# A fixed order list for every engine in place of a ranked greedy scheduler, with larger first loads, moved buffers, and sums and copies made by DMA

## The chip, the core and the metric

The kernel runs on one core of a Trainium2 chip. The metric is the device time of one execution in microseconds (us). Of the core's engines, TensorE (PE) does matrix products, VectorE (DVE) element-wise work, ScalarE (ACT) functions of one operand and copies out of PSUM, and GpSimd (POOL) and SyncE (SP) mostly issue DMAs. Each engine executes its instructions strictly in the order in which they were written; it waits on semaphores for the work of the others.

## What is computed

Two independent layers share one kernel, and their outputs are joined along the last axis. All inputs are bfloat16; S = L = 2048, D = 448, 16 heads of 28, 256 states.

```python
# A: linear attention with a softmax feature map
q, k, v = split_heads(x @ wqkv)
pq, pk = q @ w_phi, k @ w_phi                     # per head, 28 x 28
phi = lambda p: concat(softmax(p), softmax(-p))
kv, z = einsum(phi(pk), v), sum(phi(pk))
a = (phi(pq) @ kv / (phi(pq) @ z + 1e-6)) @ wo

# B: state-space convolution over the sequence
dt = exp(log_dt)
P = exp(dt * (A_re + 1j * A_im) * l)              # l = 0..2047, as bfloat16
K = einsum(C, P, dt * B).real                     # (448, 2048)
y = irfft(rfft(pad(u)) * rfft(pad(K)))[:2048] + u * Dskip
out = concat(a, y)
```

## The kernel before

**The work.** Layer B sets most of it. The raw state parameters (six tensors of 448 x 256) are turned to states on partitions (`to_states`: PE transposes, ACT copies to `st`). From them come the powers `PW[k]` for steps of 32, 64, 128, 256, 512 and the table `H` of start values. The positions l are split into 50 low and 32 high parts. Eight chunks of 56 channels each go through `chunk(k)` and `table(k)`: ACT computes exponentials (`exps`, into `E`) and sines (`rot`, into `W`) for the low parts; DVE multiplies them (`damp`), negates (`neg`), and builds the high parts in `U` from `H` by repeated complex products (`hi_tables`, levels hi.1 to hi.5); PE contracts the two (`build`), and a copy out of PSUM writes the table `Ts`. `E`, `W` and `U` have two halves, one for even and one for odd chunks. `scatter_k` moves a finished group of tables (chunks 0-3, 4-5, 6-7) into `Kt` with 48 small DMAs. `kernel_spectrum` (ks) transforms `Kt` with matrices `F` that stream from memory through a ring of buffers. `signal_spectrum(b)` (us) loads sequence half b of u twice, once by `rep_rows` and once, with rows in reverse, by `pair_rows`, forms sums and differences on DVE (`ab`), transforms them with `G1` on PE, and stores the spectrum to `SUd` in device memory, from where `load_su` fetches it. `conv_group` multiplies the two spectra on DVE (prod, comb, half) and `inverse` transforms back on PE with the constants `GI`, adding `UD`, the input scaled by Dskip. Layer A (`xT`, `fold`, `key_pair`, `key_end`, `query`) fills the gaps: its key pass runs beside chunks 0 to 4, its query pass beside the later ones.

**The order.** Every operation is a unit of a `Plan`: the engines that may run it, its estimated cost, what it reads and writes. `Plan.run` then plays the whole program with these costs. At each step it takes the engine that can start soonest and, of the units that could start there within 0.02 us, the one with the lowest number in `RANKS`, a table by label. `PHASES` keeps ACT's exponentials and sines apart, since a change of function loads a table. Copies out of PSUM may go to ACT or DVE, some DMAs to SP or POOL or ACT, PSUM tiles to one of two rings: the simulated race decides. What comes out is one list of instructions per engine.

**Lines and names used below.** All DVE two-operand instructions are issued in one helper (L429), activations in another (L442), copies in L446 (ACT only) and L452 (either engine), matrix products in L462, DMAs in L477; so the profile's groups are told apart by shape. `ua` and `ab` hold the loaded and the summed signal; `SUs`, `SKs`, `GI`, `UD`, `RING` are the late buffers and share bytes with earlier ones (`oU`, `oE`, `oPID`, `oF`, `oW` are the offsets).

Of the kernel before, what the change touches and what calls it, by code (L numbers as in the profile page):

```python
# [94 lines left out]
def rep_rows(x2, row, a, t):  # L95
    rs = x2.ap[0][0]
    return bass.AP(tensor=x2.tensor, offset=x2[row + 256 * t + 128 * (1 - a), 0].offset,
                   ap=[[2 * rs, 64], [1, D_MODEL]])

def pair_rows(x2, row, t, col):  # L100
    rs = x2.ap[0][0]
    return bass.AP(tensor=x2.tensor, offset=x2[row + 1023 - 128 - 256 * t, col].offset,
                   ap=[[128 * rs, 2], [-2 * rs, 64], [1, D_MODEL]])

RANKS = {"in": 5, "inAre": 52, "inAim": 281, "inCre": 30, "inBre": 135, "inCim": 122, "inBim": 213, "inx0": 266,
         "inx1": 145, "inx2": 100, "inx3": 168, "inqk": 114, "inG": 265, "inv_": 282, "one": 93, "pid": 190, "bd":
# [42 lines left out]
class Plan:  # L149


    LAT = {"PE": 0.28, "DVE": 0.15, "ACT": 0.16, "POOL": 0.2, "SP": 0.0}
    SLACK = 0.02
    WINDOW, COLUMNS = 3.4133, 3030

# [4 lines left out]
    def step(self, label, base, phase=None):  # L160

        self.now, self.base = label, self.ranks.get(label, base)
        return self.phases.get(label, phase)
# [68 lines left out]
    def run(self):  # L232
# [24 lines left out]
        def ring(x):  # L257

            best = None
            if x.need:  # L260
                return None
# [902 lines left out]
```

## Time and profile before

| | us |
|---|---|
| three runs | 336.96, 340.40, 339.19 |
| median | 339.19 |
| the profiled execution | 341.56 |
| its span, first to last instruction | 339.8 |
| mean granted TensorE clock in it (share of full) | 0.947 |
| DMA traffic in the span | 32.87 MB |

An execution of the profile is read in three ways here: by stages (busy time of each engine in a stretch of the span), by groups (all instructions of one line and shape: count, busy time in sum, mean in ns, idle time of the engine just before them), and in order of time (start, length, engine, line, what it writes and reads, and in brackets the idle time before it and who ended it). The mean of a group can be longer than busy time over count, since instructions of one engine overlap at their ends. For DMAs the queues' names are SPq, ACTq and POOL. Instructions that only issue DMAs are not counted as busy time on SP and ACT.

The page's row of DMA activity, in 40 equal slices (tenths of the 16 DMA engines' time):

```profile
DMA  8993001121020011200203031225369766589014
```

The first four slices (to 34 us) carry the first loads, the right third the `F` stream, the scatters and the stores.

### The profile page before, as it was taken

Reading aid. Unit: us, or ns where it says so; the run is one execution under the profiler, and the core shown is the slowest. Engines: PE = TensorE matmul, PEld = TensorE weight load, DVE = VectorE, ACT = ScalarE, POOL = GpSimd, SP = SyncE. Lnnn points to the kernel's source line nnn. Section 1 sums busy time; section 2 is a strip of 40 time slices with the busy share of each in tenths; the row PEclk is TensorE's granted clock in tenths of the full one; section 3 lists DMA queues with packets and bytes.
Section 4 is the critical chain, followed back from the end, with each engine's and each line's share of the span. In section 5 each row is a group of like instructions: output and inputs, shape, how many; then the busy total and the mean of one; then the engine's idle time right before and its main releaser. Section 6 shows DMA issues by size and latency. Waiting matters only on the chain. (4 is left out here: it accounts for less than half of the span.)

```text
span 339.8 us, 9802 instructions
## 1 busy us (share of the span) xinstructions
PE 266.4 (78%) x4193; PEld 211.0 (62%) x4193; DVE 295.0 (87%) x337; ACT 256.0 (75%) x486; POOL 48.5 (14%) x95
## 2 busy tenths in 40 slices
PE   1465766889877978989989989998679970699993
PEld 1355444546754745657777766796557960599983
DVE  0369999999999995999999999999999649959991
ACT  2789999999997978999999998999973200152420
POOL 3000000100010000000019400006900027500000
PEclk9999995999999997999999999999979976599998
DMA  8993001121020011200203031225369766589014
GB/s 164 281 303 85 0 2 50 48 84 64 31 88 23 4 56 54 109 3 3 77 12 28 10 95 43 71 70 139 54 168 245 204 194 139 132 265 246 6 56 164
DMA packets 42540, 32.87 MB, mean 97 GB/s; under 512 B 20993, under 2 KB 41890, under 8 KB 42112
## 3 DMA queue, kind: packets, MB, share of 16 engines
q1 hardware_dynamic: 36643, 30.41, 30.7%
q0 software_dynamic: 2624, 0.64, 2.0%
q10 hardware_dynamic: 3229, 1.19, 1.9%
q8 instruction: 33, 0.54, 0.7%
q14 instruction: 11, 0.09, 0.1%
HBM read 24.28 MB, written 7.34 MB: 93 GB/s over the span
## 5 line engine op out<-in xcount | busy, mean ns | idle before, releaser
L462 PEld LDWEIGHTS <-sbuf 128*32 128x32 bf16 (+5 forms) x4049 | 196.6, 122 | 99.7 <-issue 47.4
L429 DVE TENSOR_TENSOR sbuf<-sbuf 128x448 bf16<-128x448 bf16 (+9 forms) x225 | 234.4, 1085 | 24.6 <-ACT sbuf L446 13.9
L462 PE MATMUL mm<-sbuf 128*32 128x50 bf16 (+9 forms) x1923 | 146.0, 285 | 24.2 <-ACT sbuf L452 12.5
L442 ACT ACTIVATE sbuf<-arg 128x448 bf16<-128x448 f32 (+3 forms) x216 | 114.6, 709 | 0.7 <-PE arg L462 0.5
L462 PE MATMUL kb<-sbuf 128*32 128x50 bf16 (+7 forms) x1416 | 78.4, 255 | 23.7 <-DMA sbuf<-const 13.2
L452 ACT CAST sbuf<-mm 128x448 bf16<-128x448 f32 (+3 forms) x81 | 48.0, 611 | 30.3 <-PE mm L462 21.2
L477 POOL DMA_DIRECT2D sbuf<-sbuf x73 | 41.1, 590 | 108.5 <-ACT sbuf L452 41.9
L462 PE MATMUL arg<-sbuf 128*128 128x112 bf16 (+1 forms) x710 | 45.6, 220 | 0.8 <-DVE sbuf L429 0.5
L452 ACT CAST sbuf<-kb 128x448 bf16<-128x448 f32 (+4 forms) x42 | 23.4, 579 | 22.2 <-PE kb L462 20.6
L442 ACT ACTIVATE sbuf<-mm 128x448 bf16<-128x448 f32 (+1 forms) x60 | 31.0, 598 | 3.1 <-PE mm L462 2.8
L442 ACT ACT_TABLE_LOAD x14 | 18.0, 1283 | 6.3 <-DMA sbuf<-in_B_A_re_dram 6.0
L641 PE MATMUL kb<-sbuf 128*112 128x128 bf16 x64 | 8.2, 286 | 11.5 <-ACT sbuf L452 6.2
L822 DVE TENSOR_REDUCE sbuf<-sbuf 128x64 f32<-128x1792 bf16 x8 | 16.1, 2012 | 0.0
L641 PEld LDWEIGHTS <-sbuf 128*112 128x112 bf16 x64 | 7.6, 191 | 13.4 <-issue 8.6
L442 ACT ACTIVATE sbuf<-sbuf 128x896 f32<-128x896 f32 (+1 forms) x11 | 12.3, 1127 | 0.3 <-DVE sbuf L429 0.3
L429 DVE TENSOR_TENSOR sbuf<-kb,sbuf 128x448 bf16<-128x448 f32 (+3 forms) x23 | 11.8, 531 | 0.7 <-PE kb L462 0.7
L452 DVE CAST sbuf<-kb 128x448 bf16<-128x448 f32 (+2 forms) x6 | 3.6, 605 | 9.5 <-PE kb L462 9.4
L452 DVE CAST sbuf<-mm 128x448 bf16<-128x448 f32 (+4 forms) x18 | 10.5, 594 | 1.5 <-PE mm L462 1.2
L452 ACT COPY sbuf<-kb 112x512 bf16<-112x512 bf16 (+1 forms) x16 | 9.0, 602 | 3.4 <-PE kb L641 3.2
L452 ACT CAST sbuf<-arg 128x224 bf16<-128x224 f32 (+1 forms) x12 | 4.3, 396 | 9.0 <-PE arg L462 9.0
L569 PE MATMUL mm<-sbuf 112*128 112x112 bf16 x48 | 5.5, 295 | 5.9 <-ACT sbuf L442 2.6
L766 ACT ACTIVATE sbuf<-sbuf 128x1680 bf16<-128x1680 bf16 x6 | 9.8, 1641 | 0.0
(33 smaller groups left out, 70.5 us busy)
## 6 DMA issues: line engine op xcount, KB each, us to landing
sbuf<-const SPq DMA_DIRECT2D x36, 224.0 KB
SUd<-sbuf SPq DMA_DIRECT2D x16, 224.0 KB
sbuf<-const SPq DMA_DIRECT2D x3, 1024.0 KB
sbuf<-in_A_x_dram SPq DMA_DIRECT2D x4, 448.0 KB
out_dram<-sbuf SPq DMA_DIRECT2D x16, 112.0 KB
sbuf<-in_B_u_dram SPq DMA_DIRECT2D x4, 448.0 KB
sbuf<-SUd SPq DMA_DIRECT2D x2, 896.0 KB
sbuf<-SUd SPq DMA_DIRECT2D x1, 1792.0 KB
```

The costliest lines, as they stand in the source:

```text
L429: lambda: nc.vector.tensor_tensor(out=at(out_), in0=at(a), in1=at(b), op=op), [whose(a), whose(b)], [out_])
L442: lambda: nc.scalar.activation(at(out_), at(a), func, scale=scale, bias=bias),
L452: lambda e: (nc.scalar.copy if e == "ACT" else nc.vector.tensor_copy)(at(out_), at(a)), [whose(a)], [out_])
L462: nc.tensor.matmul(out_, lhsT=lhsT, rhs=rhs, start=start, stop=stop, **kw)
L477: plan.add({e: own[e] for e in engs}, lambda e=engs[0]: QUEUES[e].dma_start(out=out_, in_=in_), r, w, lat=lat, load=pieces / 16000 * max(2 ...
L569: mms(p, [lambda t, nch=nch, j=j: nc.tensor.transpose(t[:, nch, 112 * j:112 * j + 112], raw[nm][:, j, 128 * nch:128 * nch + 128], id112) f ...
L641: mms(p, [lambda t, j=j, x=x: nc.tensor.transpose(t[:, j, :], x[:, 112 * j:112 * j + 112], ident[:, :]) for j in range(4)], 0.4, [x, ident ...
L766: lambda en: nc.scalar.mul(m, m, -1.0) if en == "ACT" else nc.vector.tensor_scalar_mul(m, m, -1.0), [m], [m])
L822: plan.add({"DVE": 1.93}, lambda: nc.vector.tensor_reduce(zk, EK.rearrange("p i s (h f) -> p (i s h) f", f=D_HEAD), axis=AX.X, op=ALU.add) ...
```

## The change

- `Plan.run` no longer simulates. `ORDER` lists all 1389 units by number with one letter for the engine (P, V, A, G for POOL, S), in the order in which they are written; `PLACES` names the PSUM ring of each of 291 tiles. Ranks, phases and costs no longer choose anything. In the new list ACT makes nearly all copies out of PSUM (24 casts on DVE become 8), POOL issues 92 of the 144 scatter pieces (73 before), and six DMAs that ACT issued at the start become one.
- First loads: the raw state tensors are loaded with four neighbouring rows per partition (2048 contiguous bytes instead of 512), x likewise (3584 instead of 896). Rows then sit at other places, so `to_states` picks every fourth column, and the store of layer A's output takes every fourth row.
- `to_states` uses plain matrix products with the identity into float32 PSUM; for the two A tensors DVE multiplies straight out of PSUM by dt, with no copy between.
- `signal_spectrum`: per half two row loads go straight into `ab[:, 0]` and four pair loads into `ua`; one DVE instruction of 1792 columns forms the difference, and a DMA of POOL adds `ua` onto `ab[:, 0]` in place (`accum_op`). Before, four steps of three loads and two DVE instructions of 448 columns each.
- `hi_tables`: the copy of `H` into the first rows of `U` is a DMA; the first product reads `H` itself.
- Homes: `SU0` moves from `U` to `H`; `SU2`, `SK0`, the products `Y`, the sums `S` and a temporary `s2` move; the `F` ring has seven slots of 1792 bytes per partition (six before), of which two lie in a buffer of the key pass.

```diff
-def rep_rows(x2, row, a, t):
+def rep_rows(x2, row, a):
     rs = x2.ap[0][0]
+    return bass.AP(tensor=x2.tensor, offset=x2[row + 128 * (1 - a), 0].offset, ap=[[2 * rs, 64], [256 * rs, 4], [1, D_MODEL]])
...
-def pair_rows(x2, row, t, col):
+def pair_rows(x2, row, t):
     rs = x2.ap[0][0]
+    return bass.AP(tensor=x2.tensor, offset=x2[row + 1023 - 128 - 256 * t, 0].offset,
                    ap=[[128 * rs, 2], [-2 * rs, 64], [1, D_MODEL]])
...
+ORDER = ("0A 15G 22P 23A 24A 1S 2S 27P 28V 25P 26V 36A 16G 6S 3S 4S 29P 30V 31P 32V 37V 33A 35A 38A 34A 165S 59P 60V 12S "
+         "139P 140V 39V 166S 164S 167S 44A 43A 40A 41A 51P 57P 58V 123P 18G 143P 5S 163S 162S 124V 52V 144V 168V 45V 9S "
...
     def run(self):
+        places, done = iter(PLACES), set()
+        for word in ORDER.split():
+            u, e = self.units[int(word[:-1])], ENGINES[word[-1]]
+            assert e in u["costs"] and u["deps"] <= done
             for x in u["ps"]:
                 if x.t is None:
+                    x.make(TAGS[next(places)])
             if len(u["costs"]) > 1:
                 u["fn"](e)
             else:
                 u["fn"]()
+            done.add(u["n"])
...
-        dma(["SP", "ACT"], raw[nm][:, :, :], srcs[nm].rearrange("(j p) n -> p j n", p=112), w=[raw[nm][:, :, :]])
+        dma(["SP"], raw[nm][:, :, :], srcs[nm].rearrange("(p j) n -> p j n", j=4), w=[raw[nm][:, :, :]])
...
-            acopy(states(st[nm])[:, nch], (p, lambda t, nch=nch: channels(t[:, nch, 0:D_MODEL])))
+            p = ps("mm", [128, 512])
+            mms(p, [lambda t, j=j: mm(t[:, j:D_MODEL:4], raw[nm][:, j, 128 * nch:128 * nch + 128], id112, True, True)
+                    for j in range(4)], 0.375, [raw[nm][:, :, :], ident[:, :]], act=392)
+            use(nch, (p, lambda t: channels(t[:, 0:D_MODEL])))
...
-        tt(f[:, :], st[nm][:, :], dtx[:, :], ALU.mult)
+        to_states(nm, 10 + i, lambda nch, a: tt(states(f)[:, nch], a, states(dtx)[:, nch], ALU.mult))
...
-            tt(ab[:, 0, t, :], ua[:, 0, :], ua[:, 1, :], ALU.add)
-            tt(ab[:, 1, t, :], ua[:, 0, :], ua[:, 1, :], ALU.subtract)
+            dma(["SP"], ua[:, t, :], pair_rows(u2, 1024 * b, t), w=[ua[:, t, :]], lat=5, cost=0.85)
+        step(f"ab{b}.0", rank)
+        tt(ab[:, 1], ab[:, 0], ua[:, :, :], ALU.subtract)
+        step(f"ab{b}.1", rank)
+        dma(["POOL"], ab[:, 0], ua[:, :, :], r=[ab[:, 0], ua[:, :, :]], w=[ab[:, 0]], lat=5, cost=0.85, accum_op=ALU.add)
...
-        copy(u[:, 0:4], H[:, :, :, cols], 0.41e-3)
+        dma(["SP", "POOL"], u[:, 0:4], H[:, :, :, cols], r=[H[:, :, :, cols]], w=[u[:, 0:4]])
...
-    SUs = [group_tile("SU", i, o) for i, o in enumerate((oU, oE + 14336, oPID + 29184))]
-    SKs = [group_tile("SK", i, o) for i, o in enumerate((oF + 7168, oU + 14336, oU + 21504))]
+    SUs = [group_tile("SU", i, o) for i, o in enumerate((oH, oE + 14336, oW + 36288))]
+    SKs = [group_tile("SK", i, o) for i, o in enumerate((oF + 5376, oU + 14336, oU + 21504))]
...
-    oY, oS, oTT = oPID, oPID + 14336, (oE, oW + 21952)
-    RING = [oF + 1792 * i for i in range(4)] + [oEND, oEND + 1792]
+    oY, oS, oTT = oU, (oPID, oPW), (oE, oW + 21952)
+    RING = [oF + 1792 * i for i in range(3)] + [oEND, oEND + 1792, oEK, oEK + 1792]
```

The list's order at the places that the prediction speaks of, by counting the units in the order of the code: SP starts with the identity, the raw states Are, Cim, Aim, Cre, a pair load, Wqk, three pair loads, Bre, two row loads of u, a quarter of x, Bim. DVE's thirteenth unit is the difference of u's first half, followed by the products cs32 and cs128. ACT's copy of the power 128 (pw128) follows the copies of Bre, two of x and Bim. DVE has hi.5's two sums between the two products of damp7, then skip0 and the first product of conv0. PE runs the two builds of table 7, then the rest of the queries, mixed with the spectra of groups 0 and 1 and the first inverse; then group 2's spectra, and the inverses of the three groups.

More of the change, by code (lines that the diff above doesn't have):

```diff
@@ L182, in add @@
     def add(self, costs, fn, r=(), w=(), phase=None, lat=None, gate=None, mode=0, load=0, act=None):
[L184 to L185 removed]
+        u = dict(costs=costs, fn=fn, n=len(self.units), deps=set(), ps=[])
         self.units.append(u)
@@ L190, in add @@
                     if x not in u["ps"]:
-                        if not x.users and x.order is not None:
-                            self.orders.setdefault(x.tags[0], []).append((x.order, len(self.units), x))
                         u["ps"].append(x)
@@ L232, in run @@
-    def run(self):
-        units = self.units
-        left, table, wire, lanes = {}, None, 0.0, {True: [0.0] * 8, False: [0.0] * 8}
-        free = {e: 0.0 for e in self.LAT}
-        ready = {e: [] for e in self.LAT}
-        pe = {"warm": False, "win": -self.WINDOW, "act": 0.0, "mode": 0}
-        for u in units:
-            u["wait"], u["at"] = len(u["deps"]), 0.0
-            for m in u["deps"]:
-                units[m]["kids"].append(u)
-            if u["phase"] is not None:
-                left[u["phase"]] = left.get(u["phase"], 0) + 1
-        for u in units:
-            if not u["wait"]:
-                for e in u["costs"]:
-                    ready[e].append(u)
-        turn = {tag: [x for _, _, x in sorted(o, key=lambda z: z[:2])] for tag, o in self.orders.items()}
-        for u in units:
-            for x in u["ps"]:
-                if not x.long:
-                    for m in u["deps"] - x.users - x.need:
-                        x.need.add(m)
-                        units[m].setdefault("opens", []).append(x)
[L257 to L261, printed above, removed]
-            if x.order is None or turn[x.tags[0]][0] is x:
-                for tag in x.tags:
-                    r = self.rings.setdefault(tag, [])
-                    if len(r) < x.bufs or not r[-x.bufs].users:
-                        t = r[-x.bufs].end if len(r) >= x.bufs else 0.0
-                        if best is None or t < best[0]:
-                            best = (t, tag)
-            return best
-        def start(u, e, first):
-            t = max(u["at"], free[e])
-            for p in (u["gate"], u["phase"]):
-                if p is not None and p > first:
-                    return None
@@ L276, in start @@
+    def run(self):
+        places, done = iter(PLACES), set()
+        for word in ORDER.split():
+            u, e = self.units[int(word[:-1])], ENGINES[word[-1]]
+            assert e in u["costs"] and u["deps"] <= done
             for x in u["ps"]:
                 if x.t is None:
-                    place = ring(x)
-                    if place is None:
-                        return None
-                    t = max(t, place[0])
-            return max(t, lanes[e == "POOL"][-8]) if u["load"] else t
@@ L317, in run @@
                 u["fn"]()
-            free[e] = t + cost
-            end = t + cost + (u["lat"] or self.LAT[e])
-            if u["load"]:
-                wire = max(wire, t + 0.5 * cost + 0.25) + u["load"]
-                end = max(wire + 1.1, t + cost + (u["lat"] or 0.0))
-                lanes[e == "POOL"].append(end)
-            for x in u["ps"]:
-                x.users.discard(u["n"])
-                x.end = max(x.end, end)
-            for x in u.get("opens", ()):
-                x.need.discard(u["n"])
-            for v in u["kids"]:
-                v["wait"] -= 1
-                v["at"] = max(v["at"], t + cost if e == "PE" and e in v["costs"] else end)
-                if not v["wait"]:
-                    for k in v["costs"]:
-                        ready[k].append(v)
+            done.add(u["n"])
+        assert len(done) == len(self.units)
 class Ps:
@@ L603 @@
     for i, nm in enumerate(RAW[2:]):
-        to_states(nm, 20 + i)
+        to_states(nm, 20 + i, lambda nch, a: copy(states(st[nm])[:, nch], a))
     step("cb", 24)
```

117 lines of the change are left out of this document (33 added, 84 removed), and 103 rows, old and new, of tables (ORDER, PHASES, RANKS).

## The prediction

> **What bounds the kernel now.** I read the page first, then the stretches of the span, then the head and the tail in order of time.
>
> ```profile
> span 339.8 us, 9802 instructions
> PE 266.4 (78%) x4193; PEld 211.0 (62%) x4193; DVE 295.0 (87%) x337; ACT 256.0 (75%) x486; POOL 48.5 (14%) x95
> ```
>
> ```profile
> 0.00:27.00 27.00, 11.31 (x97) 9.51 (x98) 10.35 (x13) 17.15 (x29) 3.55 (x11) 1.00 0.95 253
> 27.00:247.00 220.00, 184.78 (x2862) 136.57 (x2862) 212.18 (x260) 211.66 (x405) 31.84 (x61) 0.97 0.18 49
> 247.00:252.10 5.10, 3.62 (x26) 2.61 (x23) 5.10 (x4) 5.10 (x8) 0.05 (x1) 0.78 0.43 105
> 252.10:331.00 78.90, 63.37 (x1147) 59.18 (x1148) 66.14 (x62) 21.73 (x49) 13.06 (x23) 0.87 0.61 168
> 331.00:339.80 8.80, 3.30 (x68) 3.14 (x64) 1.28 (x3) 0.33 (x1) 0.00 (x0) 0.90 0.50 165
> ```
>
> The columns are busy PE, PEld, DVE, ACT, POOL, then clock, DMA share, GB/s. DVE at 87% is an average over three stages. In the head (to 27) the DMA engines are full (0.95) and DVE is idle 27 - 10.35 = 16.7 us, ACT 9.9. In the middle both DVE and ACT are full: idle 7.8 and 8.3 of 220. In the tail ACT is nearly done, and PE and DVE alternate, idle 15.5 and 12.8 of 78.9. The border is the last damping product:
>
> ```profile
> 242.66 4.32 ACT L442 ACTIVATE sbuf<-arg 128x448 bf16<-128x448 f32 x9
> 245.88 9.17 DVE L429 TENSOR_TENSOR sbuf<-sbuf 128x3360 bf16<-128x3360 bf16 x5
> 248.00 19.43 DVE L429 TENSOR_TENSOR sbuf<-sbuf 128x7616 bf16<-128x7616 bf16 x19
> L429 DVE TENSOR_TENSOR sbuf<-sbuf 128x7616 bf16<-128x7616 bf16 x8 | 32.9, 4115 | 0.0
> ```
>
> ACT's last sine (chunk 7) ends at 247.0, DVE's long product of that chunk runs 248.0 + 4.1 = 252.1. Call that T0: table 7 (build7), and so the last scatter, cannot start before it. From T0 to the end are 87.7 us. So the sum is T0 plus tail.
>
> **Work of DVE and ACT.** From the new list I count which engine has each copy.
>
> ```profile
> L452 DVE CAST sbuf<-mm 128x448 bf16<-128x448 f32 (+4 forms) x18 | 10.5, 594 | 1.5 <-PE mm L462 1.2 <-DMA SUd<-sbuf 0.2
> L452 DVE CAST sbuf<-kb 128x448 bf16<-128x448 f32 (+2 forms) x6 | 3.6, 605 | 9.5 <-PE kb L462 9.4 <-issue 0.2
> L452 DVE COPY sbuf<-sbuf 128x896 bf16<-128x896 bf16 x4 | 1.5, 389 | 0.9 <-PE kb L462 0.8
> L452 ACT COPY sbuf<-sbuf 128x896 bf16<-128x896 bf16 x4 | 4.6, 1141 | 0.0
> L429 DVE TENSOR_TENSOR sbuf<-sbuf 128x448 bf16<-128x448 bf16 x64 | 22.1, 378 | 1.1 <-DMA sbuf<-in_B_u_dram 0.8
> L429 DVE TENSOR_TENSOR sbuf<-sbuf 128x1792 bf16<-128x1792 bf16 x36 | 38.4, 1079 | 0.3
> L446 ACT COPY sbuf<-mm 128x448 bf16<-128x448 bf16 x12 | 5.6, 547 | 0.1
> L452 ACT CAST sbuf<-mm 128x448 bf16<-128x448 f32 (+3 forms) x81 | 48.0, 611 | 30.3 <-PE mm L462 21.2 <-DMA out_dram<-sbuf 4.3 <-DMA SUd<-sbuf 1.9
> L766 ACT ACTIVATE sbuf<-sbuf 128x1680 bf16<-128x1680 bf16 x6 | 9.8, 1641 | 0.0
> ```
>
> DVE: 24 PSUM casts (14.1 us) become 8 (about 4.3): -9.8. The eight copies of H into U go to DMA: -1.5 here, -4.6 on ACT. Sixteen sums and differences of 448 columns (16 x 0.345 = 5.5) become two of 1792 (2.1) and two accumulating DMAs: -3.4. Small items (more xT copies and one negation onto DVE, four PSUM products for two) +1.7. Together -13, so 282. ACT: of the 12 state copies four vanish (products read PSUM) and three go to DVE, 7 x 0.47 = -3.3; H copies -4.6; a negation and two xT copies -2.8; but 19 casts (24 less the 5 of the 8 left that aren't state copies) arrive, 19 x 0.6 = +11.4. ACT stays at about 257. So DVE gets slack in the middle and ACT alone is its bound: less DVE work does not shorten it.
>
> **Head.** ACT now issues one DMA instead of six, and the raw states load in runs of 2048 bytes instead of 512.
>
> ```profile
> 6.03 1.28 ACT L442 ACT_TABLE_LOAD   x1 [6.03 <-DMA sbuf<-in_B_A_re_dram]
> 4.87 0.93 PE L569 MATMUL mm<-sbuf 112*128 112x112 bf16 x8 [2.28 <-DMA sbuf<-in_B_C_re_dram]
> 2.00:3.00 1.00, 0.53 (x1) 0.00 (x0) 0.20 (x1) 0.00 (x0) 1.00 (x2) 1.00 0.52 128
> 6.00:7.00 1.00, 0.00 (x0) 0.00 (x0) 0.00 (x0) 0.97 (x1) 0.00 (x0) 1.00 1.20 207
> 24.00:25.00 1.00, 0.31 (x4) 0.23 (x3) 1.00 (x2) 0.99 (x2) 0.00 (x0) 1.00 0.97 386
> 29.00:30.00 1.00, 0.38 (x4) 0.38 (x4) 1.00 (x2) 1.00 (x3) 0.00 (x0) 1.00 0.12 43
> 57.00:57.50 0.50, 0.50 (x3) 0.21 (x1) 0.50 (x2) 0.50 (x3) 0.00 (x0) 0.50 0.13 47
> L442 ACT ACTIVATE sbuf<-sbuf 128x896 f32<-128x896 f32 (+1 forms) x11 | 12.3, 1127 | 0.3 <-DVE sbuf L429 0.3
> L429 DVE TENSOR_TENSOR sbuf<-sbuf 128x1792 bf16<-128x1792 f32 x3 | 6.0, 2016 | 0.0
> ```
>
> POOL's own DMA issues (ns, smallest, median, largest), their time to landing (us), and SP's waits on DVE (sum, times, longest):
>
> ```profile
> L477 POOL DMA_DIRECT2D sbuf<-sbuf x73: 502/594/713, 176.8 to 293.4; - x73
> DMA to landing us min/median/max: 1.5/3.0/6.5
> SPq L477 <- DVE sbuf L429: 47.7, 5, 28.8
> ```
>
> The first table load moves from 6.0 to about 1.3. But DVE's thirteenth instruction is now the difference of all of ua0, which needs all four pair loads. A pair load runs on 2 of 16 DMA engines: share 0.13 = 2/16 at 47 GB/s, and the head of before ends with the same two engines alone (0.12, 43). Before, two pair loads lay in the head; now four lie ahead of most loads. Each of the two engines must move, up to the last load that the difference needs: four raw states 57 KB, four pair loads 229, Wqk 50, Bre 14, two row loads 28: 380 KB at 23.5 GB/s = 16 us. Data flows from about 2.2 (the row from 2 to 3), and the least landing is 1.5, so DVE's difference starts at 20. Bounds: the same loads are 2.9 MB, which all 16 engines would move by 15 at the head's 253 GB/s and by 11 at 386; 22 if the raw states go at the rate of the 207 row. I take 20, since the two-engine row is the same transfer. DVE cannot pass the difference: behind it stand the products of the powers and everything after. Then 1.1 for it and 2 x 2.0 for the products cs32 and cs128: 25.1, and ACT, which has run its sines by 16.3 (first product near 5, nine instructions near 1 us, one table load), waits for the Bre and Bim copies and then for pw128 until 25.1. By 26.8 ACT has done about 17.8 us, idle 9.0 against 9.9. So the head gives ACT 0.9 us, DVE about 3.5.
>
> [...]
>
> **T0.** Behind the last sine the list has 60 copies and 10 issues of ACT, about 33 us of work (59 copies at 0.59, of which 13 have half the columns, and one negation of 1.6), against 5.10 + 21.73 + 0.33 = 27.2 before. So ACT's work up to the last sine is 257 - 33 = 224 against 228.8: 4.8 less. From the last sine to T0 DVE now has two sums of hi7 between its two products of chunk 7: 0.2 + 1.9 + 0.7 + 4.1 = 6.9 instead of 5.1 (1.9 is the step from 245.88 to 248.00 less a start). With the same idle time in the middle: 252.1 - 0.9 - 4.8 + 1.8 = 248.2, say 248. The middle's idle time can vanish (-8) or double (+8).
>
> The two accumulating DMAs: the trace has none; POOL's rows above bound issue and landing. They move 448 KB, 1.8 us more at 253 GB/s: 3 to 8.3. ACT first needs one (copy of us0.1) after 5.3 us of its own work behind pw128, PE about as late; issued at 21, landed by 30, needed at 32. Without that cover ACT would lose what is late, one for one. The copies of H are needed only in hi.2, behind three instructions of hi.1 (1.08 + 2 x 0.35 = 1.8) that read H itself; seven of the eight are SP's, and the list puts them one to two chunks ahead. Each costs 0 to 3.0 (a landing that starts only at hi.1 would leave 1.2); I take 0, as U's half is free a chunk earlier.
>
> **Tail.** SU0 goes to H's home, free after hi7.1, instead of U's even half, free after build6 (the load at 265.39 below).
>
> ```profile
> 265.39 0.57 SPq L477 DMA_DIRECT2D sbuf<-SUd  x1
> 277.25 0.53 DVE L452 CAST sbuf<-kb 128x350 bf16<-128x350 f32 x1 [4.23 <-PE kb L462]
> 277.69 23.67 DVE L429 TENSOR_TENSOR sbuf<-sbuf 128x7168 bf16<-128x7168 bf16 x12
> 290.96 0.65 PE L462 MATMUL kb<-sbuf 128*128 128x112 bf16 x5 [9.95 <-DMA sbuf<-const]
> 269.56 3.36 PE L462 MATMUL kb<-sbuf 128*32 128x50 bf16 x128 [0.20 <-DVE sbuf L429]
> 308.84 3.61 PE L462 MATMUL mm<-sbuf 128*128 128x224 bf16 x36
> 328.82 1.94 PE L462 MATMUL arg<-sbuf 128*128 128x112 bf16 x36 [0.53 <-DVE sbuf L429]
> 334.34 0.62 DVE L452 CAST sbuf<-kb 128x448 bf16<-128x448 f32 x1 [1.14 <-PE kb L462]
> ```
>
> Before, the first large product starts at 277.7, 25.6 after T0, behind build7's copy on DVE; now that copy is ACT's and the product stands at T0 + 2. PE's work behind T0 by the list: two builds of 112 matmuls 5.9; 144 inverse matmuls of 224 columns 14.4; 288 of 112 columns 15.5; 256 spectrum matmuls 13.8 and three late units of group 0 1.8; the rest of the queries about 8: 59. DVE's 50 instructions there: 66.1 before less the casts and what now stands ahead of T0, about 57. Behind the last inverse come a copy (0.6) and the store (339.8 - 335.0 = 4.8). PE alone gives 59 + 5.4 = 64, DVE 57 + 8.8 = 66; they wait for each other at the ends of conv1 and conv2 (2 to 3 us each) and for the F loads once. I allow 6: 72. Bounds: 66 without a wait, 82 if PE stands as long as in the tail before (15.5). The scatter of group 2 (29 issues of POOL at 0.59 = 17, ten of ACT, nine of SP) ends near T0 + 28 and is needed by PE near T0 + 32, so it is covered by 4 us; the constants GI (2 MB, 8 us at 253 GB/s) are asked for when chunk 6's table is built, and needed 14 us after T0.
>
> **Sum.** 248 + 72 = 320 span. The profiled run had 341.56 for a span of 339.8, so 321.8; it lay 2.4 over the median of 339.19: **319 us**, own range 307 to 334 (middle 8 either way, tail 66 to 82, not all at once).
>
> **Rivals.** (a) The pair loads don't hold the head (they spread, or land in order): difference at 13 between the bounds 11 and 15, T0 7 earlier, 312. For it: no row shows when a load of SP lands; against it the two rows of share 0.12 and 0.13. (b) The tail stays at 87.7, since F loads still stop PE (9.95 in one wait above, and the ring has only seven slots for six): 335. Against: that wait stood behind a late SU0 and a late scatter, which the list moves. (c) Slower: SP, which now carries the H copies in a fixed place behind waiting transfers, delivers them late, and DVE stands in hi.2 of each chunk. SP's waits on DVE average 47.7/5 = 9.5. DVE has 282 - 57 = 225 us of work ahead of T0 and 13 idle in the head, so 10 us of slack; eight delays of d cost 8d - 10. Over 3.7 us each the gain is eaten, and at 6, between the landing of 3.0 and the 9.5, it gives 357. Against: the list puts most of them far ahead of their use. (d) POOL's issues, now 92 scatters instead of 73 and the two sums, are held by DVE instructions. At 2 us for each of the 29 of the last scatter it ends 58 later and the time is about 360: T0 + 85 for the scatter, 5 for two spectra, 13 for the last products, 9 for the end. Against: 73 issues under a DVE over 95% busy took 502 to 713 ns. [...]
>
> **Chances.** Forecast 0.65, (a) 0.18, (b) 0.09, (c) 0.06, (d) 0.02. Range 305 to 336: it takes in (a), (b) and both ends of the middle's idle time with the tail's. A measurement of this kernel tells about 1% from no change. Faster: 0.62 + 0.18 + 0.03 of (b) = 0.83. Same: 0.03 + 0.05 = 0.08. Slower: (c), (d) and the rest 0.09.
>
> **What would show it.** DVE's first 128x1792 difference near 20 (step head; at 13 it is (a)); ACT idle about 9 us by 27; last sine near 241 and the end of the last 128x7616 near 248; DVE casts 8; no wait over 3 us on SP's copies in hi.2; the first 128x7168 product about 2 us after T0; end about 72 after T0. The prediction is wrong if T0 stays at 252 or later, or if PE again stands 10 us for F.

## The result, and the profile after

| | before | after |
|---|---|---|
| median, us | 339.79 (336.96 to 343.10, 4 runs) | 315.38 (311.93 to 318.80, 4 runs) |
| ratio, 95% interval | 1 | 0.927 (0.915 to 0.940) |
| the profiled execution, span | 341.56, 339.8 | 315.22, 313.4 |
| table 7's build starts | 269.56 | 244.68 |
| from there to the end | 70.2 | 68.7 |

The kernel is 24.4 us faster; the forecast was 319 with a range of 305 to 336. The ratio leaves out the slowest run of each kernel (343.10 before, 318.80 after), 1.8% and 2.2% above its fastest. The page's first rows, after:

```profile
span 313.4 us, 9768 instructions
PE 257.9 (82%) x4193; PEld 206.2 (66%) x4193; DVE 281.5 (90%) x307; ACT 253.3 (81%) x492; POOL 58.9 (19%) x110
```

The stages after (columns as in the prediction: busy PE, PEld, DVE, ACT, POOL, then clock, DMA share, GB/s). The border is now the last damping product, which runs from 240.13 to 244.2; the rows are cut just behind it:

```profile
0.00:27.00 27.00, 12.20 (x70) 10.11 (x71) 11.07 (x15) 14.27 (x19) 3.29 (x10) 1.00 0.74 214
27.00:240.00 213.00, 184.89 (x3071) 139.34 (x3070) 208.90 (x242) 211.03 (x415) 38.96 (x71) 0.98 0.32 83
240.00:244.60 4.60, 3.94 (x40) 3.19 (x40) 4.56 (x3) 4.60 (x10) 0.00 (x0) 1.00 0.96 307
244.60:305.00 60.40, 54.11 (x962) 50.97 (x962) 55.69 (x47) 22.38 (x51) 16.60 (x29) 0.97 0.60 156
```

DVE's sum is the forecast 282. The head became worse for ACT, not better: it is idle 27 - 14.27 = 12.7 us there (9.9 before). DVE's idle time there hardly changed, 15.9 (16.7 before). The middle has almost no idle time left, ACT 2.0 and DVE 4.1 of 213.

The prediction split the span at the last damping product. The same view reads better when it is cut at the matrix products of table 7's build (build 7). The cut, and the column "build 7" below, is the row from which nearly all of its products run without a long wait; before, four of its 224 products already stand at 269.06. First before, then after:

```profile
0.00:269.56 269.56, 215.48 (x3285) 161.91 (x3286) 243.59 (x295) 240.12 (x450) 35.44 (x72) 0.97 0.30 81
269.56:339.80 70.24, 50.90 (x908) 49.09 (x908) 51.46 (x43) 15.86 (x36) 13.06 (x23) 0.87 0.54 156
```

```profile
0.00:244.68 244.68, 201.06 (x3181) 152.72 (x3181) 224.61 (x258) 229.98 (x441) 42.26 (x81) 0.99 0.38 102
244.68:313.40 68.72, 56.85 (x1014) 53.50 (x1014) 56.94 (x50) 23.36 (x52) 16.60 (x29) 0.95 0.58 157
```

Of the 26.4 us of span, 24.9 lie ahead of build 7 and 1.5 behind it. Ahead of it DVE has 19.0 us less work (243.59 to 224.61): 13.5 are gone from the kernel, 5.5 stand behind the build now. Its idle time fell by 5.9. ACT has 10.1 less work ahead of the build and 14.7 less idle time: before, it had ended its sines at 247.0, and from the end of the last damping product (252.1) to build 7 it was busy for only 6.2 of 17.5 us, while DVE, busy for 16.0 of them, still ran the high parts of chunk 7. Behind the build DVE does 5.5 us more than before and PE 6.0, in 1.5 us less time. PE's mean granted clock over the profiled execution also rose, from 0.947 to 0.979; what that alone brings was not separated.

### The profile page after: what moved, and what is told of

The parts are those of the page before. It is cut to its first block, busy times and chain, and to the rows that moved or that the text cites. A ratio compares the mean times of both kernels' runs of the same rounds, so it can differ in the third digit from the quotient of the medians.

```text
span 313.4 us, 9768 instructions
## 1 busy us (share of the span) xinstructions
PE 257.9 (82%) x4193; PEld 206.2 (66%) x4193; DVE 281.5 (90%) x307; ACT 253.3 (81%) x492; POOL 58.9 (19%) x110
## 5 line engine op out<-in xcount | busy, mean ns | idle before, releaser
L374 PEld LDWEIGHTS <-sbuf 128*32 128x32 bf16 (+4 forms) x4097 | 198.6, 121 | 91.5 <-issue 43.5
L341 DVE TENSOR_TENSOR sbuf<-sbuf 128x896 bf16<-128x896 bf16 (+11 forms) x209 | 228.1, 1138 | 11.3 <-DMA sbuf<-const 7.6
L374 PE MATMUL mm<-sbuf 128*32 128x50 bf16 (+9 forms) x2701 | 169.5, 277 | 28.6 <-ACT sbuf L364 11.0
L354 ACT ACTIVATE sbuf<-arg 128x448 bf16<-128x448 f32 (+3 forms) x216 | 122.0, 721 | 0.1
L364 ACT CAST sbuf<-mm 128x448 bf16<-128x448 f32 (+3 forms) x110 | 67.4, 635 | 33.6 <-PE mm L374 28.7
L389 POOL DMA_DIRECT2D sbuf<-sbuf x95 | 55.4, 607 | 178.1 <-ACT sbuf L364 95.2
L374 PE MATMUL kb<-sbuf 128*128 128x224 bf16 (+9 forms) x722 | 61.7, 243 | 10.8 <-ACT sbuf L364 5.0
L341 DVE TENSOR_TENSOR sbuf<-mm,sbuf 128x448 bf16<-128x448 f32 (+2 forms) x23 | 13.1, 571 | 7.2 <-PE mm L374 7.0
L354 ACT ACTIVATE sbuf<-sbuf 128x896 f32<-128x896 f32 (+1 forms) x11 | 11.6, 1098 | 0.0
L354 ACT ACTIVATE sbuf<-kb 112x512 bf16<-112x512 f32 x18 | 11.2, 700 | 0.0
L358 ACT CAST sbuf<-sbuf 128x1792 bf16<-128x1792 f32 (+1 forms) x5 | 7.4, 1472 | 4.1 <-DVE sbuf L341 4.1
```

The costliest lines, as they stand in the source:

```text
L341: lambda: nc.vector.tensor_tensor(out=at(out_), in0=at(a), in1=at(b), op=op), [whose(a), whose(b)], [out_])
L354: lambda: nc.scalar.activation(at(out_), at(a), func, scale=scale, bias=bias),
L358: plan.add({"ACT": 0.09 + count(out_) * 0.833e-3}, lambda: nc.scalar.copy(at(out_), at(a)), [whose(a)], [out_])
L364: lambda e: (nc.scalar.copy if e == "ACT" else nc.vector.tensor_copy)(at(out_), at(a)), [whose(a)], [out_])
L374: nc.tensor.matmul(out_, lhsT=lhsT, rhs=rhs, start=start, stop=stop, **kw)
L389: plan.add({e: own[e] for e in engs}, lambda e=engs[0]: QUEUES[e].dma_start(out=out_, in_=in_, **kw), r, w, lat=lat, load=pieces / 16000 * ...
```

## The experiments

Twelve kernels, each against the kernel before on its own chip. The table gives the median, the ratio with its interval, and from the profiled execution the start of build 7 and the stretch from there to the end.

| kernel | us | ratio (95%) | build 7 | to the end |
|---|---|---|---|---|
| pair loads on POOL | 310.41 | 0.914 (0.907 to 0.920) | 240.10 | 68.6 |
| H copies by DVE | 315.69 | 0.927 (0.919 to 0.936) | 246.83 | 68.3 |
| H copies by ACT | 325.18 | 0.955 (0.950 to 0.961) | 253.85 | 69.6 |
| 16 key copies to DVE | 335.43 | 0.986 (0.981 to 0.992) | 263.55 | 69.8 |
| raw states in 512-byte runs | 317.79 | 0.934 (0.928 to 0.941) | 246.78 | 72.7 |
| hi7 behind damp7 | 324.17 | 0.954 (0.949 to 0.958) | 254.35 | 66.8 |
| greedy planner, all else new | 425.65 | 1.248 (1.243 to 1.254) | 351.13 (first products 345.02) | 73.3 |
| old list, hi7 first | 350.16 | 1.028 (1.022 to 1.033) | 277.34 | 70.5 |
| the same, neg6 ahead of neg7 | 346.68 | 1.019 (1.013 to 1.024) | 277.05 | 65.6 |
| old list, hi7 first, 14 copies to ACT | 354.03 | 1.039 (1.034 to 1.044) | 282.76 | 70.9 |
| pairs of both halves on POOL, late difference | 314.01 | 0.925 (0.919 to 0.930) | 245.10 | 70.0 |
| the same, negations on POOL | 332.28 | 0.975 (0.970 to 0.980) | 263.93 | 67.0 |

The last column stays between 65.6 and 73.3 while the time goes from 310 to 426: nearly all of what sets these kernels apart lies ahead of build 7.

The other two columns are one execution each, and executions differ. The first difference of u's halves on DVE (the row that the head is read by) starts at 23.10 in the changed kernel, but at 24.81, 23.48, 23.70 and 23.23 in the kernels with H copies on DVE, on ACT, the key copies and hi7, whose edits do not touch the head. So a single row can move by 1.7 us without a cause in the edit. Counted from that difference, build 7 follows after 221.6 us in the changed kernel, 221.5 with the pair loads on POOL, 221.6 with 512-byte runs, 222.0 and 230.4 with H copies on DVE and ACT, 239.9 with the key copies and 231.1 with hi7.

**Do the pair loads hold the head?** The four pair loads of u's first half are issued by POOL instead of SP.

```diff
-            dma(["SP"], ua[:, t, :], pair_rows(u2, 1024 * b, t), ...)
+            dma(["SP", "POOL"], ua[:, t, :], pair_rows(u2, 1024 * b, t), ...)
-ORDER: 165S ... 166S 164S 167S
+ORDER: 165G ... 166G 164G 167G
```

> The changed kernel with the four pair loads of u's first half issued by POOL instead of SP, all else as it is. Theory 1 (two of the 16 DMA engines, loaded with all four pair loads, hold the head; issued by POOL each load lands on two other engines): the first difference on DVE, at 23.1 in the changed kernel, comes at 13 to 17; the DMA share no longer falls to 0.13 between 10 and 14; the time falls by 5 to 9 us. Rival (the head is held by the number of bytes, or POOL's loads meet on the same two engines): the difference stays at 21 or later, and the time within 2 us.

The head of the changed kernel in windows of 2 us, and in order of time what PE and DVE wait for:

```profile
10.00:12.00 2.00, 0.43 (x5) 0.43 (x6) 0.25 (x1) 2.00 (x3) 0.00 (x0) 1.00 0.13 47
12.00:14.00 2.00, 2.00 (x17) 2.00 (x16) 1.66 (x3) 1.99 (x3) 0.00 (x0) 1.00 0.14 47
16.00:18.00 2.00, 0.00 (x0) 0.00 (x0) 0.00 (x0) 0.00 (x0) 0.00 (x0) 1.00 1.09 247
```

```profile
20.81 1.67 PE L374 MATMUL mm<-sbuf 112*128 112x112 bf16 x8 [6.38 <-DMA sbuf<-in_B_B_re_dram]
23.10 6.97 DVE L341 TENSOR_TENSOR sbuf<-sbuf 128x1792 bf16<-128x1792 bf16 x5 [7.62 <-DMA sbuf<-const]
```

For 4 us the DMA share is 0.13 and 0.14, the time of about two of the 16 engines (47 GB/s); then the engines are full (1.09, 247 GB/s), but nothing that PE, DVE or ACT could use has landed, and all three stand. The difference starts at 23.10 after 7.62 us of idle time. The view names a constant's load, issued last, as what ended that wait; the difference itself reads only the pair and row loads of u. SP's own rows show why nothing else is loaded meanwhile:

```profile
4.28 7.41 SPq L389 DMA_DIRECT2D sbuf<-in_B_u_dram  x3
11.74 2.28 SPq L389 DMA_DIRECT2D sbuf<-in_B_B_re_dram  x1
14.07 1.34 SPq L389 DMA_DIRECT2D sbuf<-in_B_u_dram  x2
```

SP stands about 2.5 us in issuing each pair load behind the first (a raw state takes it 0.43), so it comes to Bre only at 11.74 and to the row loads at 14.07. The same rows with the pair loads on POOL:

```profile
10.00:12.00 2.00, 0.85 (x4) 0.42 (x3) 1.98 (x3) 1.32 (x2) 0.00 (x0) 1.00 1.18 212
```

```profile
3.55 0.62 SPq L391 DMA_DIRECT2D sbuf<-in_B_B_re_dram  x1
8.31 2.55 PE L376 MATMUL mm<-sbuf 112*128 112x112 bf16 x12 [2.27 <-DMA sbuf<-in_B_A_im_dram]
14.63 0.62 PE L562 MATMUL kb<-sbuf 112*112 112x112 bf16 x4 [3.77 <-DMA sbuf<-in_A_wqkv_dram]
18.56 6.96 DVE L343 TENSOR_TENSOR sbuf<-sbuf 128x1792 bf16<-128x1792 bf16 x5
240.10 2.98 PE L376 MATMUL kb<-sbuf 128*32 128x50 bf16 x112
```

The hole is gone, the difference stands 4.5 us earlier and no longer waits, build 7 follows 4.6 earlier, and the median is 5.0 lower. The two rows lie well outside the 1.7 us, though the two ratio intervals overlap. The difference comes later than the 13 to 17 forecast, since PE now waits for Aim (2.27) and for layer A's weights (3.77), and DVE behind PE.

The share also differs while the second half's four pair loads run: with SP in the changed kernel it is 0.13 (0.13 x 16 = 2.1 engines, 46 GB/s), with POOL in the kernel with late difference below it is 0.47 (7.5 engines, 96 GB/s). The rows do not show which engines. First the row with SP, then with POOL:

```profile
55.00:60.00 5.00, 3.75 (x29) 2.18 (x28) 4.97 (x7) 5.00 (x11) 0.18 (x2) 1.00 0.13 46
34.00:37.00 3.00, 3.00 (x20) 1.61 (x19) 3.00 (x3) 2.26 (x6) 1.12 (x3) 0.66 0.47 96
```

The edit thus changes two things at once: the pair loads take a larger share of the engines, and SP is free to issue the other loads earlier (Bre at 3.55 instead of 11.74). How much of the 4.5 us each brings was not separated.

**Does the run length count?** The changed kernel with the raw states in rows of 512 bytes again.

```diff
-srcs[nm].rearrange("(p j) n -> p j n", j=4)      t[:, j:D_MODEL:4]
+srcs[nm].rearrange("(j p) n -> p j n", p=112)    t[:, 112*j:112*j + 112]
```

> The changed kernel with the raw state tensors loaded as before (runs of 512 bytes instead of 2048), nothing else. The prediction (the pair loads' two engines move 512-byte runs slower): the difference of u's first half 2 us later than 23.1, and the time 2 us longer, 317 to 318. Rival 1 (transfers of 512 bytes go at line rate): difference at 23.1, 315 to 316. Rival 2 (the raw loads spread over other engines than the pair loads' two, or ACT has slack in the head): ACT's work starts later or not at all later, within 1 us either way.

```profile
25.17 6.96 DVE L341 TENSOR_TENSOR sbuf<-sbuf 128x1792 bf16<-128x1792 bf16 x5 [8.43 <-DMA sbuf<-const]
246.78 2.83 PE L374 MATMUL kb<-sbuf 128*32 128x50 bf16 x105
```

The difference moved from 23.10 to 25.17 and build 7 from 244.68 to 246.78, 2.1 each, and the median by 2.4. But the intervals of the two ratios overlap, 25.17 is only 0.36 above the 24.81 of a kernel with an untouched head, and the edit also changes PE's part: its last eight transposes take 0.93 us instead of 1.67. So a gain of 2 us is not shown. What the traces do show is the time of the DMA engines from 4 to 10 us, in which both kernels load raw states beside others; first with 512-byte runs, then the changed kernel:

```profile
4.00:10.00 6.00, 2.39 (x20) 1.76 (x20) 3.84 (x6) 3.67 (x5) 0.00 (x0) 1.00 0.98 211
4.00:10.00 6.00, 4.22 (x20) 3.16 (x20) 3.78 (x6) 3.15 (x4) 0.00 (x0) 1.00 0.83 227
```

With the short runs the engines are busier (0.98 against 0.83) and move less (211 GB/s against 227). Per unit of share that is 211 / 0.98 = 215 GB/s against 227 / 0.83 = 273, which speaks against rival 1, as far as rows that hold other loads too can.

**Who bounds the middle?** The copies of H, a DMA in the change, are made by DVE (eight at 0.375 us, 3.0) or by ACT (eight at 1.097, 8.8).

```diff
-        dma(["SP", "POOL"], u[:, 0:4], H[:, :, :, cols], ...)
+        copy(u[:, 0:4], H[:, :, :, cols], 0.41e-3)    # all V, or all A
```

> The changed kernel with the eight copies of H into U made by DVE again (8 x 0.39 = 3.1 us of DVE), just ahead of hi.2, and not by DMA. Theory 1 (the prediction: ACT alone bounds the middle, DVE has slack): within 1 us. Theory 2 (DVE's own work ahead of the last table bounds it): 2.5 to 3.5 us slower, table 7's product later by as much.

> The changed kernel with the eight copies of H into U made by ACT (8 x 1.14 = 9.1 us of ACT), just ahead of hi.1. Theory 1 (ACT alone bounds the middle): 7 to 9 us slower. Theory 2 (DVE alone bounds it): within 2 us. If both are full, as the busy time of both in the middle says (211.0 and 208.9 of 213), this one is slower by 7 to 9 and the copies on DVE by about 3.

On DVE they cost next to nothing: +0.3 in the median, and 0.4 in the way from the first difference to build 7 (that the table has build 7 2.2 later is mostly the head of that execution). On ACT they cost 9.8 in the median, and 8.8 in that way, for 8.8 of work. The middle stage with the copies on ACT:

```profile
27.00:240.00 213.00, 179.55 (x2812) 134.54 (x2811) 200.29 (x230) 209.35 (x402) 38.09 (x70) 0.97 0.25 63
```

ACT is as full as before and DVE is the one with slack (12.7 of 213). So work added to ACT bounds the middle of the changed kernel, as forecast. That less work on ACT would shorten it, no kernel here shows.

Then the other way: the 16 copies of the key pass that write V (0.6 us each) go from ACT to DVE, each at its place in the list.

```diff
-ORDER: <unit>A    # the 16 casts of a key tile out of PSUM into V
+ORDER: <unit>V
```

> The changed kernel with the sixteen copies of V in the key pass moved from ACT to DVE at the same places of the list (DVE +16 x 0.6 = 9.6 us, ACT -9.3). Theory 1 (ACT alone bounds the middle): up to 9 us faster. Theory 2 (DVE alone): 6 to 10 us slower. Both full: slower by 6 to 10, with ACT then waiting.

```profile
27.00:240.00 213.00, 173.78 (x2731) 127.33 (x2730) 200.16 (x236) 187.07 (x360) 29.94 (x54) 0.94 0.26 65
```

Twenty us slower, more than either theory gave: ACT is idle 25.9 and DVE 12.8 of 213, neither is full. My reading is that the copies now stand in DVE's list behind long products, PE waits for the tiles that they should free, and ACT for PE: 16 copies of 0.6 us (9.6 in sum) cost 20 us in this list. Which of the 16 does the damage was not tried.

**Is it where DVE's work stands?** On DVE's list the levels 2 to 5 of chunk 7's high parts (two of 3.2 us, two of 1.8) go back behind chunk 7's damping.

```diff
-V: ... 1011 1013 1012 1014 ... 1020 1190(damp7) 1022 1021 1191(damp7) 1284(skip0)
+V: ... 1190(damp7) 1191(damp7) 1011 1013 1012 1014 ... 1020 1022 1021 1284(skip0)
```

> The changed kernel with one thing put back on DVE's list: the twelve instructions of chunk 7's high parts from level 2 on (two levels of 3.2 and two of 1.8 us, 10.0 in sum) stand behind the two damping products of chunk 7, where the kernel before had them. Theory 1 (a gain of the list is that this DVE work lies beside ACT's last sines instead of behind them): DVE waits some 8 us for the sines, damping ends at 243 to 245 as before, table 7's build starts 10 later, at 253 to 255, and the end stays 69 behind it: 323.5 to 326 us. Rival (what counts is the sum of DVE's work ahead of the build, in whatever order): within 2 us of 315.4.

DVE and PE around the border, first in that kernel, then in the changed kernel:

```profile
237.41 1.91 DVE L343 TENSOR_TENSOR sbuf<-sbuf 128x3360 bf16<-128x3360 bf16 x1 [3.30 <-ACT sbuf L356]
240.07 19.96 DVE L343 TENSOR_TENSOR sbuf<-sbuf 128x7616 bf16<-128x7616 bf16 x15 [0.76 <-ACT sbuf L356]
254.35 2.97 PE L376 MATMUL kb<-sbuf 128*32 128x50 bf16 x112 [9.77 <-DVE sbuf L343]
```

```profile
234.51 5.59 ACT L354 ACTIVATE sbuf<-arg 128x448 bf16<-128x448 f32 x12
236.59 13.40 DVE L341 TENSOR_TENSOR sbuf<-sbuf 128x1792 bf16<-128x1792 bf16 x7
244.68 2.80 PE L374 MATMUL kb<-sbuf 128*32 128x50 bf16 x105
```

Put back, DVE waits for the sines (3.30, 0.76) and then does 10 us while PE stands 9.77 for it: build 7 9.7 later, the median 8.8. In the changed kernel the last sines end at 240.1, and behind them DVE has only a product of 4.1 before the build can start; ahead of it in that group are the last product of hi7, the first damping product and two sums, behind it skip0 and the first 128x7168 product.

The same move in the old kernel does not help. Its own order was written as a list, and the last levels of chunk 6 and all of chunk 7 moved ahead of chunk 7's damping.

```diff
-V: ... 1210(damp7) 937 1211(damp7) 938 1324(skip1) 939 940 1028 ... 1042
+V: ... 937 938 939 940 1028 ... 1042 1210(damp7) 1211(damp7) ... 1318 1324(skip1)
```

> The kernel before, its own order written as a list, with one edit: the last products of the high parts of chunks 6 and 7 (17 us of DVE) stand ahead of chunk 7's two damping products instead of behind them, and skip1 (2.0) stands behind skip0. Theory 1 (what counts is DVE's whole work ahead of build 7, which the swap leaves): build 7 at 267 to 269 instead of 269.6, damping of chunk 7 ending only just before it; 336 to 339 us. Rival (the step from the last damping product to the end, 87.7 before and 68.8 after, is shortened by this order itself): 330 or less.

ACT's list had chunk 7's negation ahead of chunk 6's; it now waited for the late damping (14.07), held chunk 6's negation, and so build 6:

```profile
259.30 1.60 ACT L751 ACTIVATE sbuf<-sbuf 128x1680 bf16<-128x1680 bf16 x1 [14.07 <-DVE sbuf L414]
```

With the two put in order:

```diff
-A: ... neg7 ... neg6 ... (build 7)
+A: ... (damp6) neg6 ... neg7 (build 7)
```

> The kernel before as a list with the same move made there: levels 4 and 5 of chunk 6 and all of chunk 7's high parts ahead of chunk 7's damping, skip1 behind skip0, and ACT's negation of chunk 6 ahead of that of chunk 7 (in the first such kernel ACT stood 14 us at the negation of chunk 7 with that of chunk 6 behind it). Theory 1 (DVE has no idle time there to fill, so only skip1 and a little waiting are won): build 7 at 263.5 to 268, the end 70 later, 335 to 340 us. Rival (the order alone brings most of the gain): build 7 by 256, 328 or less.

```profile
243.40 20.36 DVE L414 TENSOR_TENSOR sbuf<-sbuf 128x448 bf16<-128x448 bf16 x21
270.42 0.53 ACT L437 CAST sbuf<-kb 128x448 bf16<-128x448 f32 x1 [8.33 <-DMA out_dram<-sbuf]
270.92 4.00 PE L447 MATMUL kb<-sbuf 128*128 128x224 bf16 x20 [5.84 <-DMA sbuf<-const]
277.05 5.21 PE L447 MATMUL kb<-sbuf 128*32 128x50 bf16 x200 [0.30 <-ACT sbuf L751]
```

DVE is done at 243.40 + 20.36 = 263.8, where theory 1 had it, but the build comes 13 later (one early part of it, as before, at 276.44): ACT now stands 8.33 us for a store of layer A and PE 5.84 for a load of F. SP's rows show what holds both:

```profile
SPq L462 <- DVE sbuf L414: 12.0, 1, 12.0
263.79 0.62 SPq L462 DMA_DIRECT2D sbuf<-SUd  x1
264.50 3.22 SPq L462 DMA_DIRECT2D out_dram<-sbuf  x1
267.81 1.84 SPq L462 DMA_DIRECT2D sbuf<-const  x4
```

The load of a spectrum of u into E stands in SP's list where it was; it has to wait until chunk 7's damping has read E, so it goes out at 263.79 (254.15 in the kernel before), after a wait of 12.0 us, and the store and the loads of F stand behind it. The other two kernels with this list show the same wait, 11.6 and 11.2. And on the first of these two kernels, with 14 copies moved to ACT as well:

```diff
-ORDER: <unit>V    # every second of DVE's 24 casts, and the last four
+ORDER: <unit>A
```

> The same edit, and 14 of the 24 casts out of PSUM that DVE made go to ACT at their places (ten ahead of the last sine, then two of group 0's spectra and the two of build 7). Theory 1: ten casts at 0.6 leave DVE ahead of build 7, and the two of the spectra with their wait of 1.2 just ahead of it, beside skip1's 2.0: build 7 near 259.5, end 70 later, 329 to 332 us. The last sine moves from 247 to 253. Rival (ACT alone bounds the middle, as the prediction said): what ACT gets it loses, 342 or more. A second rival: in fixed lists the two queues stop each other, as with the key pass's copies, so that less than half of the 10 us comes: 335 or more.

354.03, 3.9 more than without the moved copies, and DVE, with less work, ended chunk 7's damping later, at 248.33 + 20.35 = 268.7 by the same group, against 243.15 + 20.34 = 263.5 without the moved copies. So the order alone gains nothing in the old kernel, and at least part of the loss comes from an edit in lists in which everything else kept its place, SP's among them. The old order as a list without an edit was not run, and neither was the choice of engine alone.

**The new steps without the list.** The old ranked planner orders the new operations.

```diff
-        for word in ORDER.split():
...
+    # run(), RANKS and PHASES of the kernel before
```

> The changed kernel with the old ranked greedy planner in place of the list: new loads, homes, accumulating sums and H copies by DMA, but the order and the engine of every copy out of PSUM are the planner's. Theory 1 (DVE's work and the copies' engines set when table 7's build starts; the list is most of the gain): DVE and ACT lose 5 and 11 us of work by the DMA copies and sums, the planner spends them badly; build of table 7 between 258 and 266, the end 70 behind it: 328 to 336 us. Rival (loads, homes and DMA sums are most of the gain, the list only writes it down): build 7 by 252, 322 us or less.

```profile
21.46 0.58 ACT L451 COPY sbuf<-kb 112x512 bf16<-112x512 bf16 x1 [17.70 <-PE kb L638]
35.09 0.53 ACT L451 CAST sbuf<-mm 128x448 bf16<-128x448 f32 x1 [11.57 <-PE mm L461]
```

425.65, far off both numbers. The planner puts layer A's transposes and folds ahead of the states, and SP stands in the four pair loads for 10.1 us ahead of raw states: Aim's load is issued at 28.02, in the changed kernel at 2.11.

```profile
14.13 10.10 SPq L476 DMA_DIRECT2D sbuf<-in_B_u_dram  x4
```

In the first 60 us ACT gets 7.5 of work done, where it has 45.7 done in the changed kernel: a third of the 110 us that it loses on the changed kernel is there already. Its ranks and costs were made for other steps, so this says that the new steps need an order of their own, not what a tuned planner would reach.

**Can it be better still?** Two additions to the first kernel. The pair loads of both halves go on POOL, and the first difference stands behind cs32 and cs128.

```diff
-V: ... 144 168(ab0.sub) 45(cs32) 42(cs128) ...
+V: ... 144 45(cs32) 42(cs128) 168(ab0.sub) ...
```

> The changed kernel with the pair loads of both halves of u issued by POOL, and the difference of u's first half behind the products cs32 and cs128 instead of ahead of them. Theory 1 (with the pair loads spread, ACT's first wait in the head is for those products, 1.1 us behind the difference): build 7 about 1 us earlier than the 240.1 of the kernel with the first half on POOL alone, 308.5 to 310.5 us. Rival (the loads of the second half take POOL's time from scatters, or the head is held by the load of Wqk): 310 to 312.

```profile
24.78 0.96 POOL L391 DMA_DIRECT2D sbuf<-sbuf  x1 [19.43 <-DMA sbuf<-const]
31.73 3.20 POOL L391 DMA_DIRECT2D sbuf<-in_B_u_dram  x4 [5.20 <-DMA sbuf<-sbuf]
```

```profile
31.53 1.65 PE L376 MATMUL mm<-sbuf 128*128 128x448 bf16 x4 [4.49 <-issue]
```

Slower by 3.6 in the median and by 5.0 at build 7, though the two intervals overlap slightly. The accumulating sum follows the difference: issued at 24.78 (19.95 in the first kernel), it lands near 31.5, where POOL's next load waits 5.20 for it. PE starts again at the same moment, after 4.49 us for which the view names no cause; that it too waits for the sum is inferred. ACT then stands 2.99 us behind PE. This is the uncovered wait that the prediction priced one for one; what the second half's loads on POOL add was not tried apart. In that kernel, then, the negations of 1680 columns go from ACT (five) and DVE (three) to POOL.

```diff
-nc.scalar.mul(m, m, -1.0)     ORDER: 530A 658A 761A 1025A 1192A 306V 476V 923V
+nc.gpsimd.tensor_scalar_mul(m, m, -1.0)    ORDER: the same units with G
```

> That kernel with the eight negations of 1680 columns (five on ACT at 1.72 us, three on DVE at 0.59) made by POOL. Theory 1 (ACT and DVE are both full in the middle, 211 and 209 of 213; what both lose, the time loses): ACT -8.6, DVE -1.8, so DVE becomes the bound and the build comes 2 to 5 us earlier, 304 to 308 us. Rival (POOL, for which the trace has only memsets, 0.545 us for 448 columns, is slower than the cover of the negation, or stops DVE beside it): 312 or more.

The groups of the negations and of the long damping product there, with one negation and the product beside it, and then the group of that product without them:

```profile
L680 POOL TENSOR_SCALAR sbuf<-sbuf 128x1680 bf16<-128x1680 bf16 x8 | 38.8, 4846 | 79.5 <-DVE sbuf L343 79.5
L343 DVE TENSOR_TENSOR sbuf<-sbuf 128x7616 bf16<-128x7616 bf16 x8 | 41.9, 5233 | 0.0
188.58 4.43 POOL L680 TENSOR_SCALAR sbuf<-sbuf 128x1680 bf16<-128x1680 bf16 x1 [12.79 <-DVE sbuf L343]
188.85 7.03 DVE L343 TENSOR_TENSOR sbuf<-sbuf 128x7616 bf16<-128x7616 bf16 x1
```

```profile
L343 DVE TENSOR_TENSOR sbuf<-sbuf 128x7616 bf16<-128x7616 bf16 x8 | 33.0, 4121 | 0.2 <-ACT sbuf L356 0.2
```

A negation takes 4.85 us on POOL instead of 1.72 on ACT. The mean of 5.23 for the damping product mixes two cases: the three that ran beside a negation took 7.03 to 7.25 us, the other five 4.11. DVE's whole busy time rises from 282.2 to 301.6. The rival was right. The best kernel of the study is the first, 310.41.

## Why the prediction was right, step by step

- **DVE's work** 282: 281.5. **ACT's work** 257: 253.3. The counts of copies were right.
- **Head.** Right in that the pair loads take the time of about two engines (share 0.13 and 0.14 from 10 to 14 us; which engines no row shows) and that DVE cannot pass the difference (7.62 us idle ahead of it); not in how the loads behind them start. Its sum counts what the two engines have to move, as if every load were issued in time, but SP issued Bre only at 11.74 and the row loads at 14.07. So the size came out too small: 20 forecast, 23.10 measured (23.1 to 24.8 over the five kernels with this head), and ACT idle 12.7 instead of 9.0. Rival (a), that they don't hold it, falls with the kernel that issues them from POOL: 5 us faster.
- **512-byte runs.** 2 us forecast, 2.1 measured in one execution of each, which is little more than executions differ by; that the two agree may be luck. Only the engines' time speaks for an effect of the run length here (0.98 for 211 GB/s with the short runs, 0.83 for 227 with the long).
- **T0.** 248.2 forecast, 244.2 measured (the last sines end at 240.1, then a product of 4.1). The terms: ACT's work up to the last sine 224, measured 14.27 + 211.03 + 0.1 = 225.4; its idle time in the middle 8.3, measured 2.0; its head 3.7 worse; the step from the last sine 6.9, measured 4.1, because the first damping product and the two sums of hi7 run while the sines still do. Two terms too small (5.1 together) and two too large (9.1) left 4.0: that T0 came out so near is partly luck.
- **The bound.** "ACT alone bounds its middle" holds for the changed kernel (H copies: +0.3 on DVE, +9.8 on ACT). "Less DVE work does not shorten it" is half wrong. In the kernel before, build 7 waited not for T0 alone but for the DVE work behind it (16.0 us in 17.5), and only less DVE work ahead of the sines makes room to have it beside them. Putting 10 us of it back costs 8.8. The other 15 or so of the 24.9 us ahead of build 7 were not taken apart by a run: that they come from the work gone and the idle time gone is read from the sums above.
- **Tail** 72 from T0: 313.4 - 244.2 = 69.2. The size was nearly right, the reason not. I took 87.7 as the tail before, and its shortening as waits that vanish. But T0 was the wrong border there: 17.5 of the 87.7 was DVE's way from T0 to build 7. From the build on, 70.2 became 68.7. The waits did go (before, PE stood 9.95 for F in one place; in the tail after, no wait of PE exceeds 1.5), but 5.5 us of DVE's work and 6.0 of PE's came in their place. Rival (b), a tail that stays at 87.7, was a question put at the wrong border. Which part of the vanished waits is due to the new homes and the seventh slot of the ring was not tried.
- **(c)** SP's copies of H: DVE's idle time in the whole middle is 4.1, and the copies on DVE instead change the median by 0.3, so none came late enough to count. **(d)** POOL's issues under a busy DVE: the row after denies it, mean 0.607 us for 95 issues, 65 of them in the middle under a DVE busy at 98% (208.90 of 213). The rows of the kernel before did so too, 502 to 713 ns, though only 50 of the 73 issues lay under a DVE busy over 95% (67.76 of 70.2 us from 176.8 to 247; then 38.16 of 46.4, 82%).

```profile
L389 POOL DMA_DIRECT2D sbuf<-sbuf x95 | 55.4, 607 | 178.1 <-ACT sbuf L364 95.2
```

- **The accumulating sums**, bounded at 3 to 8.3 from issue to landing, take 5.8 (median of the two), covered by 2 us or less, as the kernel with the late difference suggests.

## What to carry to other kernels

Cut the span at the instruction that the tail waits for (here the first product of the last build), not at the last step of the engine that seems to be the bound; then count each engine's work and idle time ahead of the cut. Where two engines were both full, as here, work was taken from the sum and the order changed together; in a fixed list, one edit alone mostly uncovered the next wait, in SP's list too. A load that runs at a small DMA share ahead of others on the same queue is worth a look at the rows of the engine that issues it: here, at 0.13 (47 GB/s) from 10 to 12 us, SP issued the next load, Bre, only at 11.74. Before reading a shift of a row as the effect of an edit, subtract what the head of that execution brought.

## What was not expected of the hardware

A 128x1680 negation on POOL took 4.85 us, 2.8 times ACT's 1.72 and eight times DVE's 0.59, and the two-operand DVE product beside it took 7.03 to 7.25 us instead of 4.1. POOL's DMA issues did not show it: in the changed kernel the longest two-operand DVE instruction took 4.13 us, with issues of POOL (13 from 225.40 to 232.03) beside one of the 128x7616 products (in the group 228.74 to 233.94).
